# A gated mix of an S4 convolution and a dense branch, forward and backward: one row layout, the dense branch in three parts, S4 tables in place, transposes by DMA

## The chip, the cores and the metric

The kernel runs on one core of a Trainium2 chip. The metric is the device time of one execution in microseconds (us). The kernel before took 1587.69 us, the median of three runs (1584.29 to 1588.03). One execution was also recorded by the hardware profiler, and all rows below come from that one.

## What is computed

The input `u` has 2048 rows of 448 channels. A gate `g` (one number per row) mixes two branches, and the kernel returns the output and the gradients of all parameters:

```python
g = sigmoid((u * gate_w).sum(-1))
# branch a: a state-space convolution (S4), N = 256 complex modes per channel
K[d, l] = Re( sum_n  C[d,n] * exp(dt[d] * A[d,n] * l) * dt[d] * B[d,n] )
a = irfft(rfft(u padded) * rfft(K padded))[:L] + u * Dskip
# branch b: dense, 448 -> 1792 -> 448
b = relu(u @ w1 + b1)**2 @ w2 + b2
out = g * a + (1 - g) * b        # and the vjp of this for grad_out
```

The gradients need two more convolutions (`dK` from `u` and `g * grad_out`, `du` from `K` and `g * grad_out`), two sums S and T per channel and mode over the gradient `dK`, and six matrix products in place of the dense branch's two.

## The kernel before, in words

The whole program is one function of straight-line code. A planner orders the instructions of each engine before the run: the program's order is the priority, an instruction that the planner thinks ready may pass one that is not, a `high_priority` block goes ahead, and at run time each engine and each DMA queue takes its list strictly in order. Buffers come from pools. A pool that is opened after another has been closed gets the same memory, so its first use waits for the last use of the old one.

The stages, in the program's order:

1. Gate (L586 to L603) and S4 parameters (L291 to L349, transposed by TensorE). Rows of `u` lie as `(lt p)`, row `128*lt + p` on partition `p`, so `g * grad_out` goes out to DRAM and comes back in the layout of the transform.
2. Forward transforms of `u` and `g * grad_out` (`fwd1`, `fwd2`, each a set of matmuls with a trip through DRAM between, `gd`), the product of the spectra (`cmul_spec`), and the inverse (`inv1`, `inv2`, with a trip through `hd`), which gives `dK`.
3. S4 (L649 to L664): 14 chunks of 32 channels. For each pair of chunks `multipliers` makes sines and exponentials on VectorE and ScalarE. `build` then makes two tables by doubling, `Y` (6 levels) and `XW` (5 levels), each level three VectorE operations (L392 to L394). `Y` has two buffers and `build` has high priority, so the tables of chunk c+1 are made beside the use of chunk c. `kgen` makes the filter K, `back` transposes the tables on TensorE (L461, L471), copies them out of PSUM on ScalarE (L462, L474), multiplies by `dK` (L480), copies (L483), makes two products per group of channels on VectorE (L489, L490) and sums them by matmuls with a selection matrix (L499).
4. Transform of K, the parameters' gradients (L699 to L758), two products of spectra and two inverses, stored as `y_d` and `du_d`.
5. The dense branch (L780 to L932), in two halves of 896 hidden units. Its products need `h` and its gradient in both orientations, so `h` is transposed on TensorE and the hidden gradient is computed twice (L897, L908). Each half runs seven loops of matmuls one after another. Its pools are opened after the transforms' are closed.
6. The tail (L940 to L1011): loads of `grad_out`, `y_d`, `du_d`, and whole-tensor VectorE operations for output and input gradient.

All DMAs are issued from the queues of SP and ACT; POOL issues none.

Of the kernel before, what the change touches and what calls it, by code (L numbers as in the profile page):

```python
# [2 lines left out]

# [9 lines left out]
ALU = mybir.AluOpType  # L13
# [66 lines left out]
class FFTCtx:  # L80
    def __init__(self, tc, cpool, wpool, stg, psum, dram_consts=None):
        self.tc = tc
        self.nc = tc.nc
        nc = self.nc
        self.wpool = wpool
        self.stg = stg
        self.psum = psum
        if dram_consts is None:
            hc = host_consts()
            dram_consts = {name: (nc.inline_tensor(arr, name=f"c_{name}"), arr.shape) for name, arr in hc.items()}  # L90
        self.dram_consts = dram_consts
        self.c = {}
        for i, (name, (dr, shp)) in enumerate(dram_consts.items()):
            class _A:
                shape = shp
            arr = _A
            with tc.tile_pool(name=f"cld_{name}", bufs=1) as cld:
                t32 = cld.tile([P, arr.shape[1]], fp32, name=f"c32_{name}")
                (nc.sync if i % 2 == 0 else nc.scalar).dma_start(t32[:], dr.ap())
                tb = cpool.tile([P, arr.shape[1]], bf16, name=f"cb_{name}")  # L100
                nc.vector.tensor_copy(tb[:], t32[:])
            self.c[name] = tb
        self.evac_i = 0

    def dma(self):
        self.dma_i = getattr(self, "dma_i", 0) + 1
        return self.nc.sync if self.dma_i % 2 == 0 else self.nc.scalar

    def evac(self, dst, src):
        nc = self.nc  # L110
        if self.evac_i % 3 != 2:
            nc.scalar.copy(dst, src)  # L112
        else:
            nc.vector.tensor_copy(dst, src)
        self.evac_i += 1

    @staticmethod
    def tl_dram(ap2d):
        t = ap2d.tensor
        off = ap2d.offset  # L120
        return bass.AP(tensor=t, offset=off, ap=[[16 * D, 4], [64 * D, 32], [1, 16 * D]])

    def tl_load(self, dst_tile3, src_dram2d):
        for g in range(4):
            src = bass.AP(tensor=src_dram2d.tensor, offset=src_dram2d.offset + 16 * g * D, ap=[[64 * D, 32], [1, 16 * D]])
            self.dma().dma_start(dst_tile3[32 * g:32 * g + 32].rearrange("p a d -> p (a d)"), src)

    def tl_store(self, dst_dram2d, src_tile3):
        for g in range(4):
            dst = bass.AP(tensor=dst_dram2d.tensor, offset=dst_dram2d.offset + 16 * g * D, ap=[[64 * D, 32], [1, 16 * D]])  # L130
            self.dma().dma_start(dst, src_tile3[32 * g:32 * g + 32].rearrange("p a d -> p (a d)"))

    def fwd1(self, src_dram2d, gd, pool, tag="xs"):
        nc = self.nc
        c = self.c
        xs = pool.tile([P, 16, D], bf16, tag=tag, name=tag)
        self.tl_load(xs, src_dram2d)
        F1 = c["F1BD"]
        for hh in range(2):
            for q in range(4):  # L140
                st = self.stg.tile([P, 4, D], bf16, tag="st", name="st_g")
                for j2 in range(2):
                    ps = self.psum.tile([P, 2, 512], fp32, tag="ps", name="ps")
                    for jj in range(2):
                        j0p = q * 4 + j2 * 2 + jj
                        nc.tensor.matmul(ps[:, jj, 0:D], lhsT=F1[:, hh * 128:(hh + 1) * 128], rhs=xs[:, j0p, :], start=True, stop=True)
                    self.evac(st[:, 2 * j2:2 * j2 + 2, :], ps[:, :, 0:D])
                j0base = 32 * hh + q * 4
                for g2 in range(2):
                    dst = bass.AP(tensor=gd, offset=(j0base + 16 * g2) * 64 * D,  # L150
                                  ap=[[D, 64], [64 * D, 4], [1, D]])
# [890 lines left out]
```

## Time and profile before

| | before |
|---|---|
| profiled execution, device time | 1587.86 us |
| its span, first to last instruction | 1586.1 us |
| mean granted TensorE clock | 0.757 of full speed |
| median of 3 runs | 1587.69 us |

The rows give start or busy times in us, and the mean of one instruction in ns. Busy time of overlapping instructions on an engine is counted once, while the mean is of each instruction alone, so a mean times a count can exceed the busy time. A queue (SPq, ACTq) is where an engine issues DMAs. "Idle before" is how long an engine stood before such instructions, and what ended the wait.

### The profile page before, as it was taken

The page shows a single profiled execution, that of the slowest core. Times are in us where ns is not written, and L with a number is a line of the kernel's source. Part 1 is how long each engine was busy: PE and PEld are TensorE (multiplying, and loading weights), DVE is VectorE, ACT ScalarE, POOL GpSimd, SP SyncE. Part 2 cuts the span into 40 slices and gives each one's busy share as a digit, 9 for nine tenths or more (in the row PEclk, how much of TensorE's full clock was granted, in tenths as well). Part 3 has the DMA queues.
Part 4 walks back from the last instruction along what each step waited for, and adds up shares of the span by engine and source line. Part 5 has one row for each costly group of instructions (what it writes and reads, how often), then busy time and mean ns, then how long its engine had stood idle before and what let it go on. Part 6 is the DMA issues. An engine that isn't in the chain of part 4 may idle for free. (4 is left out here: it accounts for less than half of the span.)

```text
span 1586.1 us, 22870 instructions
## 1 busy us (share of the span) xinstructions
PE 860.7 (54%) x9553; PEld 500.8 (32%) x9568; DVE 1041.7 (66%) x1432; ACT 753.1 (47%) x976; POOL 38.4 (2%) x97
## 2 busy tenths in 40 slices
PE   0243410464656656575656231123499999999911
PEld 0111100343444434454444110000255455444500
DVE  3422834999999999999994269831225720766267
ACT  0033471585858586876654253113173636245042
POOL 0000000000000000000000000000000000000000
PEclk9966655577786768777887655555599999999965
DMA  6576448000000000000002753499501000000042
GB/s 148 132 239 212 202 113 187 1 2 8 2 9 1 8 2 8 2 2 8 2 8 51 195 184 133 151 121 253 170 21 33 9 21 1 1 21 6 17 139 93
DMA packets 92302, 115.53 MB, mean 73 GB/s; under 512 B 18019, under 2 KB 88678, under 8 KB 90278
## 3 DMA queue, kind: packets, MB, share of 16 engines
q1 hardware_dynamic: 52854, 57.43, 14.1%
q10 hardware_dynamic: 39344, 56.63, 11.5%
q8 instruction: 75, 1.23, 0.3%
q14 instruction: 29, 0.24, 0.1%
HBM read 65.41 MB, written 48.63 MB: 72 GB/s over the span
## 5 line engine op out<-in xcount | busy, mean ns | idle before, releaser
L499 PE MATMUL sps<-P,sel 128*32 128x256 bf16 x896 | 149.3, 323 | 70.6 <-DVE P L490 39.6
L499 PEld LDWEIGHTS <-sel 128*32 128x32 bf16 x896 | 95.0, 111 | 114.1 <-issue 88.5
L483 ACT CAST zb<-psz 128x1024 bf16<-128x1024 f32 x112 | 111.1, 1028 | 22.2 <-PE psz L480 21.9
L474 ACT COPY yts<-ytp 128x1024 bf16<-128x1024 bf16 x112 | 109.4, 1031 | 11.3 <-PE ytp L471 11.1
L433 PE MATMUL psk<-Y,XW 128*32 128x64 bf16 x1792 | 31.0, 241 | 114.2 <-DVE XW L394 112.4
L471 PE MATMUL ytp<-identb,Y 128*64 128x128 bf16 x1792 | 87.4, 243 | 8.7 <-ACT XT L462 8.7
L480 PE MATMUL psz<-yts,DK 64*32 64x256 bf16 x896 | 48.5, 368 | 68.6 <-ACT yts L474 67.6
L489 DVE TENSOR_TENSOR P<-zb,XT 128x2048 bf16<-128x2048 bf16 x56 | 68.4, 1221 | 25.3 <-ACT zb L483 25.1
L392 DVE TENSOR_TENSOR U<-Y,PRY 128x128 bf16<-128x128 bf16 (+2 forms) x84 | 72.9, 868 | 14.8 <-POOL Y L404 11.8
L471 PEld LDWEIGHTS <-Y 128*64 128x64 bf16 x1792 | 67.2, 123 | 35.4 <-issue 34.0
L394 DVE TENSOR_TENSOR Y<-U,V 128x128 bf16<-128x128 bf16 (+2 forms) x84 | 73.1, 870 | 2.2
L393 DVE TENSOR_TENSOR V<-Y,PIY 128x128 bf16<-128x128 bf16 (+2 forms) x84 | 72.4, 862 | 0.0
L394 DVE TENSOR_TENSOR XW<-U,V 128x256 bf16<-128x256 bf16 (+4 forms) x70 | 70.2, 1003 | 0.9
L392 DVE TENSOR_TENSOR U<-XW,PRX 128x256 bf16<-128x256 bf16 (+4 forms) x70 | 69.9, 999 | 0.7
L393 DVE TENSOR_TENSOR V<-XW,PIX 128x256 bf16<-128x256 bf16 (+4 forms) x70 | 69.8, 997 | 0.0
L490 DVE TENSOR_TENSOR P<-zb,XT 128x2048 bf16<-128x2048 bf16 x56 | 68.4, 1222 | 0.0
L433 PEld LDWEIGHTS <-XW 128*32 128x32 bf16 x1792 | 28.0, 124 | 120.5 <-issue 120.0
L186 PEld LDWEIGHTS <-cb_MI 64*128 64x128 bf16 x192 | 13.2, 119 | 161.5 <-issue 135.0
L186 PE MATMUL ps<-PcY,cb_MI 64*128 64x448 bf16 x64 | 14.8, 560 | 90.6 <-ACT st_h L112 36.5
L112 ACT CAST st_g<-ps 128x896 bf16<-128x896 f32 x33 | 29.0, 907 | 70.4 <-DMA gd<-st_g 38.2
L112 ACT CAST st_h<-ps 128x896 bf16<-128x896 f32 x32 | 28.0, 904 | 68.6 <-DMA hd<-st_h 47.7
L437 ACT CAST Kall<-psk 128x512 bf16<-128x512 f32 x14 | 8.2, 585 | 104.6 <-PE psk L433 104.6
(253 smaller groups left out, 2009.0 us busy)
## 6 DMA issues: line engine op xcount, KB each, us to landing
Gn<-in_grad_out_dram ACTq DMA_DIRECT2D x3, 1792.0 KB, 12.7
gd<-st_g SPq DMA_DIRECT2D x24, 224.0 KB, 3.1
gd<-st_g ACTq DMA_DIRECT2D x24, 224.0 KB, 3.9
hd<-st_h SPq DMA_DIRECT2D x12, 448.0 KB, 4.6
hd<-st_h ACTq DMA_DIRECT2D x12, 448.0 KB, 5.9
hs<-hd SPq DMA_DIRECT2D x12, 448.0 KB, 7.0
hs<-hd ACTq DMA_DIRECT2D x12, 448.0 KB, 9.4
c_M<-c_M ACTq DMA_DIRECT2D x2, 2048.0 KB, 8.2
```

The lines of the kernel that those rows point to most:

```text
L112: nc.scalar.copy(dst, src)
L392: nc.vector.tensor_tensor(out=U, in0=lo, in1=bcast_dims(pr, [0, (None, n), 1]), op=ALU.mult)
L393: nc.vector.tensor_tensor(out=V, in0=rev_dim(lo, 3), in1=bcast_dims(pi, [0, (None, n), 1]), op=ALU.mult)
L394: nc.vector.tensor_tensor(out=hi, in0=U, in1=V, op=ALU.add)
L433: nc.tensor.matmul(ps[32 * g:32 * g + 32, 0, i * 64:(i + 1) * 64], lhsT=XW[:, W2 + w, :, 1 - t], rhs=Y[:, w, :, t], start=(k == 0), stop=( ...
L471: nc.tensor.transpose(ytp[64 * t:64 * t + 64, ii, h * P:(h + 1) * P], Y[:, w, :, t], self.identb[:], tile_position=(0, 64 * t))
L474: nc.scalar.copy(yts[:], ytp[:])
L480: nc.tensor.matmul(psz[32 * ii:32 * ii + 32, t, 256 * s:256 * s + 256], lhsT=(DK[64 * t:64 * t + 64, :, d] if s == 0 else DKB[64 * t:64 * ...
L483: nc.scalar.copy(zb[:, :, :, i2, :], psz[:].rearrange("p t (s n) -> p t s n", s=2))
L489: nc.vector.tensor_tensor(out=P1[:].rearrange("p t s g n -> p t s (g n)"), in0=zv, in1=xb, op=ALU.mult)
L490: nc.vector.tensor_tensor(out=P2[:].rearrange("p t s g n -> p t s (g n)"), in0=zv, in1=rev_dim(xb, 1), op=ALU.mult)
L499: nc.tensor.matmul(sps[32 * g:32 * g + 32, r, 0:256], lhsT=self.sel[:, k, off:off + 32], rhs=Q[:, t, s, i2, :], start=first, stop=last, ti ...
```

## The change

Nearly every line is rewritten. What it does, part by part:

1. **One layout.** Rows lie as the transform wants them (partition `32*g + l1` holds the 16 rows `64*l1 + 16*g + t`) from the first load to the last store, also in the dense branch. The trip of `g * grad_out` through DRAM, `y_d` and `du_d` go. Constants come as bf16.
2. **S4 multipliers once, ahead.** For each of the 14 chunks a record of all 11 levels is made before the transforms' products, stored to DRAM and loaded again by its chunk. The first two values of each doubling come from the record, so `XW` has 4 levels and `Y` has 5.
3. **Tables in place.** `Y` and `XW` have one buffer each, for all chunks; `build(c+1)` writes where `kgen(c)`, `tables_t(c)` and the loads of chunk c read. `build` has no priority over `back`.
4. **Y transposed by DMA.** Four transposing DMAs per chunk, 512 KB each, from the SP queue, into three rotating buffers, replace 128 transposes on TensorE and eight copies on ScalarE. `kgen` and the transposes of `XW` share one PSUM bank.
5. **Dense branch in three parts.** Part 1 (hidden units and their gradient, once each, transposed layout, stored to DRAM) stands behind the first transforms in the program and must end before S4 begins, since S4's `Y` and `XW` use the memory of its inputs. Part 2 (gradients of w1 and w2, with 28 transposing loads of 512 KB from DRAM) and part 3 (output of the branch and its input gradient) stand behind S4 and the K transform in the program, but use memory and PSUM banks that are free during S4.
6. **Tail inside the inverses.** The two last inverses add the skip term, the dense branch and the gate's gradient by further matmuls into the same PSUM tile, and VectorE and ScalarE write the outputs from it.
7. **POOL issues DMAs**: records, spectra, weights, hidden units, K, S and T, the parts of the dense branch.

The core of the diff (left out: the classes `FFTCtx` and `S4`, whose bodies are shown above, the transforms, which are the same matmuls on quarters of a spectrum, and the gradients of the parameters):

```diff
-    tcp0_ctx = ExitStack()
-    T = S4(tc, tcp0)
+    UT = K.t("Y16", [P, LT, DT, P])
+    DBT = K.t("X16", [P, LT, DT, P])
+    for (dst, src) in ((UT, U), (DBT, DB)):
+        for q in range(4):
+            nc.sync.dma_start_transpose(out=dst[:, 4 * q:4 * q + 4].rearrange("p t a b -> p (t a) b"),
+                                        in_=src[:, 4 * q:4 * q + 4, :].rearrange("p t d -> p (t d)"))
+    K.fwd1(lambda j: U[:, j, 0:D], gd[0])
+    K.fwd1(lambda j: DA[:, j, :], gd[1])
...
+    for c in range(NCH):
+        tw = K.t("F17", [P, 4, NLEV, W2], fp32)
+        v, s, q_, e = (tw[:, i] for i in range(4))
+        rec = K.t("rec", [P, NF, W2])
+        V.tensor_tensor(out=v, in0=Tt[:, c]..., in1=pow2[:]..., op=ALU.mult)
+        V.tensor_scalar(out=s, in0=v, scalar1=MAGIC, scalar2=MAGIC, op0=ALU.add, op1=ALU.subtract)
+        V.tensor_tensor(out=v, in0=v, in1=s, op=ALU.subtract)
+        S.activation(s, v, ACT.Sin, scale=2 * math.pi)
+        S.activation(q_, v, ACT.Sin, scale=math.pi)
+        S.activation(q_, q_, ACT.Square)
...
+        V.scalar_tensor_tensor(out=rec[:, 0:NLEV], in0=q_, scalar=-0.5, in1=e, op0=ALU.add, op1=ALU.mult)
+        V.tensor_tensor(out=rec[:, NLEV:2 * NLEV], in0=s, in1=e, op=ALU.mult)
...
+        G_.dma_start(dst, rec[:].rearrange("p f w -> p (f w)"))
...
+    for jp in range(FT // 2):
...
+            for lc in range(4):
+                ps = K.ps(NT[nti % 4], [P, 512])
+                for dt in range(DT):
+                    T_.matmul(ps[:], lhsT=w1t[0:k, dt, jj * P:jj * P + P], rhs=UT[0:k, 4 * lc:4 * lc + 4, dt, :], ...)
+                S.activation(rT[:, 512 * lc:512 * lc + 512], ps[:], ACT.Relu, bias=b1_f[:, j:j + 1])
+            V.tensor_tensor(out=h2, in0=rT, in1=rT, op=ALU.mult)
+            G_.dma_start(bass.AP(tensor=hT_d, offset=j * P * L, ap=[[L, P], [1, L]]), h2)
...
+    Y = K.t("Y16", [P, W2, 2, 64])
+    XW = K.t("X16", [P, 2, W2, 32, 2])
+    def double(T3, n, T4, rev, pr, pi):
...
+        V.tensor_tensor(out=hi, in0=lo, in1=bcast_dims(pr, [0, (None, n // 2), 1]), op=ALU.mult)
+        V.tensor_tensor(out=Vv..., in0=lo, in1=bcast_dims(pi, [0, (None, n // 2), 1]), op=ALU.mult)
+        V.tensor_tensor(out=T4[:, :, :, n:2 * n], in0=T4[:, :, :, n:2 * n], in1=V4, op=ALU.add)
+    def tables_t(c):
+        for gp in range(2):
+            for gg in range(2):
+                pt = K.ps("X", [P, 4, 256], bf16)
...
+                S.copy(XT[:, gg].rearrange("p t i n -> p (t i n)"), pt[:].rearrange("p a n -> p (a n)"))
+    def load_yt(g):
+        YT = RB[:, 3 + yi % 3].rearrange("p (h i n) -> p h i n", h=2, i=CW)
+        nc.sync.dma_start_transpose(out=YT.rearrange("p h i n -> p (h i) n"), in_=Y[:, 16 * g:16 * g + 16].rearrange("p w t b -> p (w t b)"))
...
+    for c in range(NCH):
+        build(c)
+        kgen(c)
+        XTs = tables_t(c)
+        back(c, XTs, [load_yt(g) for g in range(3)])
...
+    for j in range(FT):
+        for w in range(2):
+            hh = hn[:, (2 * j + w) % 4]
+            nc.sync.dma_start_transpose(out=hh, in_=bass.AP(tensor=src, offset=j * P * L, ap=[[L, P], [1, L]]))
+            for t in range(LT):
+                T_.matmul(ps[:, 0:width], lhsT=hh[:, t, :], rhs=(DB2[:, t, :] if w == 0 else U[:, t, 0:D + 1]), ...)
...
+    for lb in range(LT // 2):
...
+            G_.dma_start(hb, bass.AP(tensor=(hT_d if w == 0 else dhT_d), offset=256 * lb, ap=[[L, P], [P * L, FT], [1, 256]]))
...
+            K.inv2(hs, q, x, ps, lambda t: [(ident[:], A[:, t, :]), (negI[:], BR[:, t, 0, :])])
+                V.scalar_tensor_tensor(out=jk[:], in0=ps[:, hp, 0:D], scalar=1.0, in1=Gt[:, t, :], ..., accum_out=dg[:, t:t + 1])
+                V.scalar_tensor_tensor(out=A[:, t, :], in0=ps[:, hp, 0:D], scalar=g32[:, t:t + 1], in1=BR[:, t, 0, :], ...)
```

## Rows read from the trace of the kernel before

**Rows 1.** Busy time by stage: window, us, PE, PEld, DVE, ACT, POOL, PEclk, DMA, GB/s.

```profile
0.00:80.00 80.00, 9.18 (x32) 5.16 (x32) 33.83 (x95) 5.57 (x10) 1.55 (x10) 1.00 0.58 139
80.00:262.00 182.00, 59.34 (x320) 22.46 (x320) 74.42 (x78) 78.46 (x90) 1.51 (x7) 0.59 0.61 187
262.00:878.00 616.00, 357.36 (x6720) 262.77 (x6720) 579.17 (x640) 406.17 (x444) 31.84 (x80) 0.75 0.06 13
878.00:1135.00 257.00, 64.28 (x368) 22.36 (x369) 129.04 (x215) 71.54 (x114) 0.84 (x1) 0.53 0.69 186
1135.00:1505.00 370.00, 357.91 (x2066) 183.62 (x2081) 171.77 (x370) 164.29 (x270) 2.64 (x2) 0.99 0.05 14
1505.00:1586.00 81.00, 12.65 (x49) 4.46 (x48) 53.48 (x37) 27.05 (x48) 0.00 (x0) 0.62 0.33 114
```

**Rows 2.** The chain that ended last, its shares of the span by engine (page, part 4).

```profile
PE 21%; DVE 4%; ACT 1%; DMA 1%; issue 1%; DVEq 0%; ACTq 0%
```

**Rows 3.** Busy time in one chunk of S4, columns as in rows 1.

```profile
343.00:384.00 41.00, 23.94 (x486) 18.23 (x484) 40.41 (x45) 23.53 (x27) 2.36 (x8) 0.79 0.03 8
```

**Rows 4.** Groups on VectorE during S4 by shape: busy us, mean ns, idle before.

```profile
L489 DVE TENSOR_TENSOR P<-zb,XT 128x2048 bf16<-128x2048 bf16 x56 | 68.4, 1221 | 25.3 <-ACT zb L483 25.1
...
L392 DVE TENSOR_TENSOR U<-XW,PRX 128x256 bf16<-128x256 bf16 x14 | 5.2, 371 | 0.1
...
L372 DVE TENSOR_TENSOR tA<-tB,tD 128x640 f32<-128x640 f32 x6 | 4.9, 819 | 0.0
...
L372 DVE TENSOR_TENSOR tA<-tB,tD 128x768 f32<-128x768 f32 x5 | 4.8, 959 | 2.4 <-ACT tD L371 2.4
```

**Rows 5.** Timeline within one chunk of S4: start, duration, instruction.

```profile
549.99 1.94 PE L433 MATMUL psk<-Y,XW 128*32 128x64 bf16 x128 [9.44 <-DVE XW L394]
...
551.86 1.89 PE L461 MATMUL xtp<-identb,XW 128*128 128x128 bf16 x16
...
551.99 0.59 ACT L437 CAST Kall<-psk 128x512 bf16<-128x512 f32 x1 [10.83 <-PE psk L433]
...
552.93 1.93 ACT L462 COPY XT<-xtp 128x1024 bf16<-128x1024 bf16 x2 [0.35 <-PE xtp L461]
...
557.93 0.37 PE L480 MATMUL psz<-yts,DK 64*32 64x256 bf16 x8 [0.28 <-ACT yts L474]
...
558.66 1.06 ACT L483 CAST zb<-psz 128x1024 bf16<-128x1024 f32 x1
```

**Rows 6.** DMA issues: queue, count, KB each, median us from issue to landing.

```profile
Gn<-in_grad_out_dram ACTq DMA_DIRECT2D x3, 1792.0 KB, 12.7
...
hd<-st_h SPq DMA_DIRECT2D x12, 448.0 KB, 4.6
...
hs<-hd ACTq DMA_DIRECT2D x12, 448.0 KB, 9.4
...
s_d<-stS SPq DMA_DIRECT2D x28, 64.0 KB, 1.7
```

**Rows 7.** Groups in the dense stage, 1135 to 1505 us.

```profile
L854 PE MATMUL ps<-uT,w1h 128*128 128x512 bf16 x215 | 51.7, 380 | 0.4
...
L912 DVE SCALAR_TENSOR_TENSOR r_l<-dh2b,r_l 128x448 bf16<-128x448 bf16 x64 | 39.3, 625 | 10.0 <-ACT dh2b L911 3.7
...
L856 ACT ACTIVATE rT<-ps,b_f 128x512 bf16<-128x512 f32 x56 | 37.5, 686 | 10.3 <-PE ps L854 10.1
```

**Rows 8.** Groups in the stage of the K transform, 878 to 1135 us.

```profile
L112 ACT CAST SP_K<-ps 128x896 bf16<-128x896 f32 x11 | 9.4, 910 | 0.4 <-PE ps L165 0.4
...
L527 DVE TENSOR_TENSOR cm<-SPx,SP_K 128x1792 bf16<-128x1792 bf16 x8 | 8.7, 1090 | 5.0 <-DMA SPx<-sp_d 5.0
...
L718 DVE TENSOR_TENSOR x<-Wr,ST 128x256 f32<-128x256 f32 (+1 forms) x12 | 5.1, 424 | 0.6 <-ACT ob_dBi L746 0.2
```

**Rows 9.** Groups on ScalarE, whole span: sines of the multipliers.

```profile
L367 ACT ACTIVATE tC<-tA 128x768 f32<-128x768 f32 x7 | 5.9, 844 | 0.1
```

**Rows 10.** Timeline of the first stage: the gate's first operation, and its wait.

```profile
25.51 3.89 DVE L590 TENSOR_TENSOR prod<-Un,gw_bc 128x7168 bf16<-128x7168 bf16 x1 [8.60 <-DMA Un<-in_A_u_dram]
```

More of the change, by code (lines that the diff above doesn't have):

```diff
@@ L20 @@
 P = 128
-L, D = 2048, 448
+L, D, N, F = 2048, 448, 256, 1792
+LT = L // P
+FT = F // P
+DT = 4
+DSZ = [128, 128, 128, 64]
+DP = 512
+CW = 8
+NG = 4
+CC = NG * CW
+NCH = D // CC
+GC = 2
+W2 = 2 * CC
+NLEV = 11
+NF = 26
+MAGIC = 12582912.0
 def host_consts():
@@ L512 @@
[L512 to L534 removed]
+        self.pool = pool
@@ L944 @@
-    for lt in range(LT):
-        nc.vector.tensor_scalar(out=DA_n[:, lt, :], in0=Gn[:, lt, :], scalar1=g32[:, lt:lt + 1], scalar2=None, op0=ALU.mult)
-    Yn = fin1.tile([P, LT, D], bf16)
-    nc.sync.dma_start(Yn[:], y_d.ap().rearrange("(lt p) d -> p lt d", p=P))
-    DUn = fin1.tile([P, LT, D], bf16)
-    nc.scalar.dma_start(DUn[:], du_d.ap().rearrange("(lt p) d -> p lt d", p=P))
-    row = small.tile([1, 4, D], fp32)
-    ps = psA.tile([P, 512], fp32, tag="ps", name="ps")
-    for lt in range(LT):
-        nc.tensor.matmul(ps[0:1, 0:D], lhsT=ones_b[:, 0:1], rhs=DB_n[:, lt, :], start=(lt == 0), stop=(lt == LT - 1))
@@ L955 @@
-    nc.vector.tensor_copy(row[:, 0, :], ps[0:1, 0:D])
-    with tc.tile_pool(name="tmp2", bufs=1) as tmp2:
-        dau = tmp2.tile([P, LT, D], bf16)
-        nc.vector.tensor_tensor(out=dau[:], in0=DA_n[:], in1=Un[:], op=ALU.mult)
-        ps = psA.tile([P, 512], fp32, tag="ps", name="ps")
-        for lt in range(LT):
-            nc.tensor.matmul(ps[0:1, 0:D], lhsT=ones_b[:, 0:1], rhs=dau[:, lt, :], start=(lt == 0), stop=(lt == LT - 1))
-        nc.vector.tensor_copy(row[:, 1, :], ps[0:1, 0:D])
@@ L990 @@
-    gp = small.tile([P, LT], bf16)
-    nc.vector.tensor_tensor(out=gp[:], in0=g_b[:], in1=omg_b[:], op=ALU.mult)
-    ds_b = small.tile([P, LT], bf16)
-    nc.vector.tensor_tensor(out=ds_b[:], in0=dg_b[:], in1=gp[:], op=ALU.mult)
-    ds32 = small.tile([P, LT], fp32)
-    nc.vector.tensor_copy(ds32[:], ds_b[:])
-    ps = psA.tile([P, 512], fp32, tag="ps", name="ps")
-    for lt in range(LT):
-        nc.tensor.matmul(ps[0:1, 0:D], lhsT=ds_b[:, lt:lt + 1], rhs=Un[:, lt, :], start=(lt == 0), stop=(lt == LT - 1))
@@ new lines @@
+    GU = K.t("Y16", [P, LT, D])
+    V.tensor_tensor(out=GU[:], in0=Gt[:], in1=Ut[:], op=ALU.mult)
+    row = K.t("st", [1, 3, D], bufs=2)
+    ps = K.ps("N0", [P, 512])
+    for t in range(LT):
+        T_.matmul(ps[0:1, 0:D], lhsT=omg_b[:, t:t + 1], rhs=Gt[:, t, :], start=(t == 0), stop=(t == LT - 1))
+    S.copy(row[:, 0], ps[0:1, 0:D])
+    nc.sync.dma_start(out_13.rearrange("(o d) -> o d", o=1), row[:, 0])
+    ps = K.ps("N1", [P, 512])
+    for t in range(LT):
+        T_.matmul(ps[0:1, 0:D], lhsT=g_b[:, t:t + 1], rhs=GU[:, t, :], start=(t == 0), stop=(t == LT - 1))
@@ L1015 @@
+    ps = K.ps("N0", [P, 512])
+    for t in range(LT):
+        T_.matmul(ps[0:1, 0:D], lhsT=ds_b[:, t:t + 1], rhs=Ut[:, t, :], start=(t == 0), stop=(t == LT - 1))
+    S.copy(row[:, 2], ps[0:1, 0:D])
+    nc.sync.dma_start(out_14.rearrange("(o d) -> o d", o=1), row[:, 2])
 _INS = ['A_u', 'A_A_re', 'A_A_im', 'A_B_re', 'A_B_im', 'A_C_re', 'A_C_im', 'A_log_dt', 'A_Dskip', 'B_x', 'B_w1', 'B_b1', 'B_w2', 'B_b2', 'gate_w', 'grad_out']
```

1407 lines of the change are left out of this document (619 added, 788 removed).

## The prediction

> **What bounds the kernel now.** I read the busy time by stage first [rows 1]. Six windows cover the span, and they run one after another. S4, 616 us, is VectorE's: it is busy 579 of them, and a single chunk shows 40.4 of 41.0 us [rows 3]; the chunks that follow repeat this. The dense stage, 370 us, is TensorE's (358 busy, granted clock 0.99), and VectorE and ScalarE are less than half busy in it. The two transform stages, 182 and 257 us, are nobody's: no engine is busy for more than half of either, the DMA share is 0.6 to 0.7, the clock 0.59 and 0.53, so they wait for trips through DRAM. The tail, 81 us, is a line of VectorE operations. The chain that ended last [rows 2] reaches back only through the tail and the dense stage (TensorE 21% of the span), so it says nothing of S4; I go by the windows. In each stage some engine stands idle that another stage needs, and what the change can win is overlap.
>
> The profiled execution took 1587.86 us, 1.8 us more than its span and 0.2 us more than the median of 1587.69, so a sum made against the span needs 1.8 us added and nothing more.
>
> **Part 1, up to S4 (before: 262 us).** The gate can't start before its first load lands, at 25 us [rows 10]. It becomes 16 fused operations of 0.63 us [rows 7], 10 us in place of two large ones; about 40 us with the scalings. Its scaled rows no longer go out to DRAM and back. The records are new here, and they are a chain, since `tw` and `rec` have one buffer each: five VectorE operations on 704 fp32 elements, between 0.82 and 0.96 us [rows 4], take 4.5 us; three on ScalarE, a little under 0.84 us [rows 9], 2.4 us; the small ones on the path, as an estimate, 3 us. Ten us each, 14 of them, 140 us from about 35 on: 175 us. The products of the spectra use the same memory (`F17`), so they start only then; four quarters with their inverses, each six products of 1.09 us [rows 8] and the copies behind them, need 35 us: 210 us. Dense part 1 runs beside this: 448 matmuls at 0.24 us (busy time over count [rows 7]) are 107 us, with the transforms' 59 [rows 1] 166 on TensorE. ScalarE gets 59 copies of 0.91 [rows 8], 56 activations of 0.69 [rows 7], 56 copies that I price alike, and the records' 70: 200 us. VectorE gets the records' 78, 29 copies and 24 products of 1.09, dense 36, gate 20: 192 us. Both are near full, so I add 30 us for waits: the first build starts at 240 us. Bounds: 205, where the two engines run without a gap, and 300, where the records stretch by a half. The inverse that gives `dK` ends beside the first build; if it is late, chunk 0's matmuls wait up to 20 us.
>
> **S4 (before: 616 us).** VectorE's work per chunk falls: the multipliers' five tensor operations per pair of chunks (0.96 and 0.82 us [rows 4], half of the sum 4.5 us) and the first level of each table (six of at most 0.37 us) go. From 40.4 us that leaves 34 to 35; I take 35, since means overlap. But the tables now have one buffer, and the overlap of one chunk's use with the next one's tables goes. I count from the end of `Y(c)`. `kgen` takes 1.9 us, its copy 0.6; then the `XW` transposes in four rounds through one bank, each 0.95 us for eight (16 take 1.89) and 1.0 for the copy [rows 5]: 7.8 us; then four small start values, about 1.2 us. Only at 11.5 us may VectorE write `XW(c+1)`. What it has until then are products, and the first needs a transposing load, 0.4 us of matmuls and two copies of 1.06 [rows 5].
>
> Before has no transposing DMA and so no price for one of 512 KB. The nearest rows move plain pieces: 1792 KB in 12.7 us, so 3.6 us for 512 KB, below; 448 KB to landing in 4.6 us from SBUF and in 9.4 us into SBUF [rows 6], so 5.3 and 10.7 us, above. I take 5.3, since it is the row that starts from an SBUF tile on SP's queue. [...]
>
> So the first product starts at 8.3 us, and VectorE idles for that long in each chunk: 43.3 us. The fourth load waits for a free buffer and lands by 22 us, before `XW` is done at about 30, so it costs nothing; that cover is gone once loads take over 8 us. Behind those loads stand, on SP's queue, two transposing loads of dense part 2 per chunk, and on TensorE some 64 dense matmuls; for what they hold up I add 4 us: 47 us. ScalarE loses eight copies of Y and gains little. Bounds: 38.5 us (transposes of `XW` done before `kgen`, 3.5 us of idle time) and 57 us (below). The first build costs 26 us (35 less eight products of up to 1.22 us [rows 4]). S4: 26 + 13 x 47 = 637 us.
>
> **After the last table (before: 257 + 370 + 81 us).** Dense parts 2 and 3 are 896 matmuls, 215 us at 0.24 us. TensorE was idle 17 us of each chunk [rows 3], 238 us in all, and loses the 128 transposes of Y, so I cost them at nothing here; without that cover, see the second rival. The remaining path: the last chunk's four loads 21 us; K read back in pieces of 256 bytes, 20 us (between 12.7 and 4 x 9.4 [rows 6]); first transform stage 25 us (half of its copies wait for two PSUM buffers instead of four; 16 to 35); DRAM trip 10 us; four quarters of 12 products and four copies at 1.09 us on VectorE, 17.5 us each, 70 us; last store 5 us. Parameter gradients: 4 x 31 operations at 0.42 us [rows 8], 52 us, of which I put 22 in the waits and 30 on the path. Tail: first load 9, first inverse with 32 fused operations of 0.63 us [rows 7] and waits 23, second inverse eight steps of about 4 us, 32, last store 5. Sum 151 + 30 + 69 = 250 us; bounds 190 and 338, the two windows of before [rows 1].
>
> **Sum.** 240 + 637 + 250 + 1.8 = 1129 us, 459 us less than before. The dense stage is 370 of that.
>
> **Rivals.**
> 1. *S4's gap closes.* The planner puts the `XW` transposes ahead of `kgen`, since they need only `XW`: 38.5 us per chunk, 1129 - 13 x 8.5 = 1018 us. For it: one priority order, and nothing else ready on TensorE then. Against it: the shared bank.
> 2. *The dense parts don't go under S4.* They stand behind it in the program, and if the planner finds no room or a list built on wrong durations stalls, they follow S4: 896 matmuls at 0.38 us (the mean of one, when they don't run densely [rows 7]) are 340 us from 877 on, then the load of their result 13 and the inverses 60: about 1290 us. Part 3 alone (170 us) would be hidden by the K transform.
> 3. *Queues hold S4 up.* SP's list, TensorE's and POOL's are in order: a dense transposing load or matmul whose data is late stands before a load of `Y`, a `kgen` or a record. One extra load of 10 us per chunk in the way makes 57 us: 1259 us. For it: 84 transposing loads of 512 KB on one queue; POOL's DMAs have no row at all.
> 4. *Slower: the transposing loads take their time block by block.* A load has 16 blocks of 128x128. If each cost what the smallest row shows, 1.7 us for 64 KB [rows 6], a load takes 27 us, the next `Y` (13 us) waits for four of them, and a chunk takes 121 us. With y us per load the total is 666 + 56y: 2178 us, and slower than before from y = 16.5 us, three times the price I took and half again the highest plain row. [...] Against it: the plain rows move a whole tile in the time of a few small ones, so blocks should overlap.
>
> **How the numbers follow.** Forecast 0.46, rival 1 0.13, rival 2 0.13, rival 3 0.20, rival 4 0.07; 0.01 for what I don't see. The range runs from below rival 1 to above rivals 2 and 3 with part 1 at its upper bound: 1010 to 1400 us; rival 4 is left out. A measurement of this kernel can tell about 0.3% from no change. Faster by more: 0.91; within: 0.01; slower: 0.08.
>
> **What would show it.** S4: `kgen` copies 47 us apart, with VectorE idle some 8 us ahead of the first product or of `XW`; 4 transposing loads each about 5 us. Dense matmuls of parts 2 and 3 inside S4's window, and the granted clock there above 0.75. The first build at 240 us, held by the records' chain. The prediction is wrong if a transposing load takes over 10 us, if the tail waits for the dense branch's result, or if ScalarE's list, not the records, sets the first stage.

## The result and the profile after

The changed kernel takes 1355.57 us (median of 4 runs, 1349.27 to 1360.10) against 1587.86 us: a ratio of 0.854 (95% interval 0.850 to 0.858), 232 us less. The forecast was 1129 us, 459 us less; the time lies inside its range, and the gain is half of what it stated. The profiled execution is one of 1360.10 us, with a span of 1358.3 us.

Busy time by stretch, kernel after (columns as in [rows 1]). The stretches are divided at the first build of the tables (288.5 to 328.4) and, from there on, at the copies of `kgen` (chunk 0, chunks 1 and 2, chunk 3, chunks 4 to 12, and what follows the last copy):

```profile
0.00:288.50 288.50, 183.72 (x692) 53.90 (x693) 182.86 (x315) 168.46 (x318) 46.10 (x94) 0.89 0.75 215
288.50:328.40 39.90, 8.24 (x76) 1.99 (x76) 32.39 (x32) 16.47 (x22) 2.56 (x5) 0.50 0.69 191
328.40:411.80 83.40, 47.28 (x609) 24.79 (x608) 37.52 (x35) 35.28 (x55) 5.15 (x9) 0.70 0.93 165
411.80:521.80 110.00, 91.75 (x1023) 49.20 (x1022) 74.50 (x70) 52.40 (x86) 20.38 (x34) 0.91 0.85 172
521.80:635.20 113.40, 54.66 (x512) 26.30 (x510) 37.51 (x35) 26.65 (x41) 16.96 (x24) 0.71 0.97 131
635.20:1115.90 480.70, 221.67 (x3492) 128.69 (x3491) 337.59 (x315) 192.15 (x261) 41.07 (x69) 0.65 0.39 81
1115.90:1358.00 242.10, 118.82 (x688) 38.89 (x688) 163.07 (x301) 67.02 (x84) 4.48 (x9) 0.59 0.73 189
```

The dense stage of [rows 1] is gone: its parts 2 and 3 run from 369 to 737 us, in S4's time. But S4 has become longer: VectorE, full before [rows 3], is busy 337.59 of 480.70 us in the nine chunks from 4 on, and 37.51 of 113.40 us in chunk 3 alone. The time went into waits in S4 and into a late start of it; the stretch behind S4 came out as forecast.

One of the chunks without dense work, kernel after, timeline (columns as in [rows 5]) and busy time:

```profile
950.50 2.29 DVE L555 TENSOR_TENSOR Y<-Y,F 128x4096 bf16<-128x4096 bf16 x1
952.85 1.96 PE L593 MATMUL psX<-Y,X 128*32 128x64 bf16 x128 [26.32 <-DVE Y L555]
952.94 11.14 SPq L622 DMA_TRANSPOSE R<-Y  x4
954.87 0.59 ACT L597 CAST st<-psX 128x512 bf16<-128x512 f32 x1 [3.01 <-PE psX L593]
959.22 0.47 PE L642 MATMUL psF<-R,K 64*32 64x256 bf16 x8 [4.42 <-DMA R<-Y]
959.84 1.03 PE L613 MATMUL psX<-ident,X 128*128 128x128 bf16 x8
964.98 2.36 DVE L654 TENSOR_TENSOR P<-R 128x2048 bf16<-128x2048 bf16 x2 [12.19 <-ACT R L645]
966.20 1.01 PE L613 MATMUL psX<-ident,X 128*128 128x128 bf16 x8 [0.49 <-ACT R L614]
977.56 0.42 DVE L549 TENSOR_TENSOR X<-X,F 128x512 bf16<-128x512 bf16 x1
1005.00 2.29 DVE L555 TENSOR_TENSOR Y<-Y,F 128x4096 bf16<-128x4096 bf16 x1
...
954.87:1009.37 54.50, 19.43 (x352) 11.89 (x352) 37.50 (x35) 20.64 (x27) 1.11 (x2) 0.53 0.30 49
```

`Y` ends at 952.8. The bank of the `XW` transposes is free from 955.5 on, yet they start at 959.84: on TensorE's queue they stand behind matmuls on `YT`, the transposed `Y`, which wait for the first load until 959.22. So the first product waits 12.19 us, the eight products (9.8 us of work) spread over 14 us behind the copies of ScalarE, and the next `XW` starts 25 us after `Y`'s end.

Longer stalls stand in chunk 0, in chunk 3 and at the start of chunk 4. Timelines, kernel after, of these three (four, four and three rows); in the distances between copies of `kgen` below, the last two both count as chunk 3:

```profile
328.39 14.00 SPq L622 DMA_TRANSPOSE R<-Y  x1
342.73 2.16 SPq L522 DMA_DIRECT2D K<-dk_d  x1
362.53 0.69 PE L642 MATMUL psF<-R,K 64*32 64x256 bf16 x16 [30.43 <-DMA K<-dk_d]
367.62 2.36 DVE L654 TENSOR_TENSOR P<-R 128x2048 bf16<-128x2048 bf16 x2 [39.26 <-ACT R L645]
...
522.84 28.67 SPq L802 DMA_TRANSPOSE D<-in_B_w_dram  x2
523.19 1.10 POOL L799 DMA_DIRECT2D U<-in_B_w_dram  x1
551.61 9.01 SPq L622 DMA_TRANSPOSE R<-Y  x3
562.02 2.36 DVE L654 TENSOR_TENSOR P<-R 128x2048 bf16<-128x2048 bf16 x2 [41.73 <-ACT R L645]
...
608.62 13.80 SPq L622 DMA_TRANSPOSE R<-Y  x3
626.77 4.73 PE L821 MATMUL psN<-D,S 128*128 128x448 bf16 x14 [7.53 <-DMA S<-dhT_d]
633.72 0.47 PE L593 MATMUL psX<-Y,X 128*32 128x64 bf16 x34
```

In chunk 0 `dK` lands only at 362; half of it was issued behind a transposing load that held SP's queue for 14 us. The two halves of that load, from the view of DMA issues (columns as in [rows 6]):

```profile
K<-dk_d ACTq DMA_DIRECT2D x1, 1792.0 KB, 25.8
K<-dk_d SPq DMA_DIRECT2D x1, 1792.0 KB, 19.8
```

So the hold is the smaller part of this wait: ACT's half, issued at 326.38, had 25.8 us to go by itself and landed at 352.17, 10 us ahead of SP's. In `e7`, below, both halves are issued at 319.8, behind no such hold, and take 22.5 and 25.1 us. In chunk 3 the loads of `Y` stand on SP's queue behind two transposing loads of dense part 3's weights (28.67 us of issue, a load of 1568 KB by POOL beside them). In chunk 4 `kgen`, ready at 608.5, stands on TensorE's queue behind dense matmuls whose block lands at 626.77.

The first stage, kernel after: busy time of three stretches, then the first operation and the end of the first record, the end of the last one, and the products of the first three quarters of the spectrum, each by its first operation:

```profile
0.00:40.00 40.00, 6.72 (x16) 2.07 (x17) 19.46 (x72) 6.66 (x8) 6.61 (x27) 1.00 0.99 200
40.00:80.00 40.00, 19.41 (x54) 5.35 (x53) 17.69 (x29) 14.37 (x19) 1.31 (x2) 1.00 1.00 204
160.00:200.00 40.00, 39.56 (x148) 11.38 (x146) 33.75 (x58) 37.64 (x83) 12.82 (x21) 1.00 0.58 198
...
67.17 0.88 DVE L418 TENSOR_TENSOR F<-P,pow 128x704 f32<-128x704 f32 x1
100.06 0.22 DVE L435 TENSOR_TENSOR rec<-F 128x64 bf16<-128x64 f32 x1
223.57 0.22 DVE L435 TENSOR_TENSOR rec<-F 128x64 bf16<-128x64 f32 x1
223.82 1.09 DVE L202 TENSOR_TENSOR F<-K 128x1792 bf16<-128x1792 bf16 x1
246.64 1.09 DVE L202 TENSOR_TENSOR F<-K 128x1792 bf16<-128x1792 bf16 x1 [1.72 <-ACT K L159]
264.35 1.09 DVE L202 TENSOR_TENSOR F<-K 128x1792 bf16<-128x1792 bf16 x1 [0.66 <-ACT K L159]
```

For 80 us the DMA engines are full, and no other engine is busy for half of it; by 160 us TensorE is full (39.56 of 40 us) and ScalarE nearly (37.64). The first record takes from 67 to 100 us, the other 13 take 9.5 us each. The products start as the last record ends, and a quarter takes 17.7 us (the first one 22.8).

### The profile page after: what moved, and what is told of

Its sections match the earlier page's. It is cut to its first block, busy times and chain, and to the rows that moved or that the text cites. A ratio compares the mean times of both kernels' runs of the same rounds, so it can differ in the third digit from the quotient of the medians.

```text
span 1358.3 us, 17800 instructions
## 1 busy us (share of the span) xinstructions
PE 726.1 (53%) x7088; PEld 323.8 (24%) x7088; DVE 865.4 (64%) x1102; ACT 558.4 (41%) x865; POOL 136.7 (10%) x244
## 3 DMA queue, kind: packets, MB, share of 16 engines
q1 hardware_dynamic: 252280, 96.03, 37.4%
## 5 line engine op out<-in xcount | busy, mean ns | idle before, releaser
L654 DVE TENSOR_TENSOR P<-R 128x2048 bf16<-128x2048 bf16 x112 | 133.9, 1223 | 307.4 <-ACT R L645 296.2
L645 ACT CAST R<-psF 128x1024 bf16<-128x1024 f32 x112 | 115.2, 1051 | 43.1 <-PE psF L642 34.2
L159 ACT CAST st<-psF 128x896 bf16<-128x896 f32 x69 | 60.8, 909 | 111.2 <-PE psF L220 56.1
L663 PE MATMUL psS<-P,cb_sel 128*32 128x256 bf16 x896 | 91.2, 321 | 19.5 <-DVE P L654 19.3
L614 ACT COPY R<-psX 128x1024 bf16<-128x1024 bf16 x56 | 56.9, 1015 | 58.3 <-PE psX L613 58.2
L555 DVE TENSOR_TENSOR Y<-Y,F 128x256 bf16<-128x256 bf16 (+4 forms) x70 | 70.5, 1007 | 2.4
L549 DVE TENSOR_TENSOR Y<-Y,F 128x256 bf16<-128x256 bf16 (+4 forms) x70 | 70.4, 1006 | 1.9
L550 DVE TENSOR_TENSOR F<-Y,F 128x256 bf16<-128x256 bf16 (+4 forms) x70 | 69.7, 995 | 0.4
L549 DVE TENSOR_TENSOR X<-X,F 128x512 bf16<-128x512 bf16 (+3 forms) x56 | 64.8, 1158 | 1.9 <-ACT F L567 0.5
L550 DVE TENSOR_TENSOR F<-X,F 128x512 bf16<-128x512 bf16 (+3 forms) x56 | 64.5, 1151 | 1.9 <-ACT F L568 1.9
L555 DVE TENSOR_TENSOR X<-X,F 128x512 bf16<-128x512 bf16 (+3 forms) x56 | 64.8, 1156 | 1.4
L663 PEld LDWEIGHTS <-cb_sel 128*32 128x32 bf16 x896 | 52.4, 109 | 54.4 <-issue 45.0
L161 DVE CAST st<-psF 128x896 bf16<-128x896 f32 x27 | 29.4, 1089 | 51.0 <-DMA gd<-st 26.4
L613 PE MATMUL psX<-ident,X 128*128 128x128 bf16 x448 | 52.7, 291 | 11.7 <-ACT R L614 10.7
L220 PE MATMUL psF<-P,cb_MI 64*128 64x448 bf16 x128 | 28.8, 560 | 56.1 <-DVE P L204 25.1
L642 PE MATMUL psF<-R,S 64*32 64x256 bf16 x896 | 57.5, 365 | 0.5 <-ACT S L631 0.5
```

The costliest lines, as they stand in the source:

```text
L549: V.tensor_tensor(out=hi, in0=lo, in1=bcast_dims(pr, [0, (None, n // 2), 1]), op=ALU.mult)
L550: V.tensor_tensor(out=Vv.rearrange("p (x a q) -> p x a q", x=rows, q=2), in0=lo, in1=bcast_dims(pi, [0, (None, n // 2), 1]), op=ALU.mult)
L555: V.tensor_tensor(out=T4[:, :, :, n:2 * n], in0=T4[:, :, :, n:2 * n], in1=V4, op=ALU.add)
L613: T_.transpose(pt[:, 2 * t + i2, h * P:(h + 1) * P], XW[:, t, w:w + 4, :, 0].rearrange("p w a -> p (w a)"), ident[:])
L614: S.copy(XT[:, gg].rearrange("p t i n -> p (t i n)"), pt[:].rearrange("p a n -> p (a n)"))
L642: T_.matmul(psz[32 * ii:32 * ii + 32, t, 256 * s:256 * s + 256], lhsT=(DK[64 * t:64 * t + 64, :, d] if s == 0 else DKB[64 * t:64 * t + 64, ...
```

## The experiments

Each kernel differs from the changed kernel by the edit shown. Only the changed kernel and `e12_all` were run four times; every other time is of a single run, so the table goes by stretches of the traces: the first copy of `kgen`, the distances from one such copy to the next (us), and the rest of the span. Chunk 3 is noisy: in `e3`, `e4`, `e10` and `e11`, whose edits lie elsewhere, it took 80 to 96 us, not 113. I count no difference in it as a gain of theirs. The start varies too: in `e11`, whose edit lies behind S4, the records end at 237 us instead of 224 and the first copy comes 14 us late. And the first two columns go together: in `e1` the matmuls of the first `kgen` end at 330.6 as before, but its copy stands on ScalarE's queue behind an operation that waits for `dK` until 359.8. The wait that the changed kernel has in chunk 0 lies ahead of the first copy in `e1`, so the two columns are to be compared by their sum (411.8 us in the changed kernel, 407 in `e1` and `e2`, 394 to 397 in `e7` to `e9` and `e12`).

| kernel | time | first | chunk 0 | 1, 2 | 3 | 4 to 12, mean | rest |
|---|---|---|---|---|---|---|---|
| changed, profiled | 1360.1 | 330 | 81 | 56, 54 | 113 | 53.4 | 242 |
| e1_xw_early | 1289.0 | 362 | 46 | 54, 47 | 77 | 51.1 | 242 |
| e2_xw_pipelined | 1268.8 | 362 | 45 | 48, 49 | 75 | 49.1 | 245 |
| e3_records_first | 1317.2 | 327 | 70 | 56, 59 | 80 | 53.3 | 244 |
| e4_bulk_beside_loads | 1357.3 | 332 | 81 | 54, 55 | 86 | 55.9 | 245 |
| e5_part3_paced | 1291.5 | 332 | 79 | 53, 55 | 52 | 52.8 | 243 |
| e6_y_by_tensore | 1285.3 | 330 | 72 | 48, 48 | 72 | 51.4 | 251 |
| e7_ordered | 1240.5 | 351 | 45 | 47, 49 | 81 | 46.5 | 247 |
| e8_ordered_paced | 1227.1 | 351 | 44 | 50, 47 | 62 | 46.0 | 257 |
| e9_ordered_tensore | 1162.0 | 351 | 43 | 39, 41 | 40 | 42.8 | 262 |
| e10_quarters_ahead | 1318.6 | 316 | 80 | 56, 55 | 89 | 52.7 | 247 |
| e11_no_param_grads | 1334.5 | 344 | 80 | 54, 55 | 96 | 52.9 | 227 |
| e12_all | 1162.6 | 358 | 39 | 40, 41 | 42 | 42.2 | 261 |

**The order on TensorE's queue.**

```
     for c in range(NCH):
-        build(c)
-        kgen(c)
+        rec = build_x(c)          # the levels of XW
         XTs = tables_t(c)
+        build_y(rec)              # the levels of Y
+        kgen(c)
         back(c, XTs, [load_yt(g) for g in range(3)])
```

> Edit: the sixteen transposes of XW and their four copies are written between the building of XW and the building of Y, so they no longer stand on TensorE's queue behind the first matmuls on YT; nothing else changes. Theory A (in the chunks without dense work, 53.5 to 54.5 us each, VectorE waits 12 us for its first product because the XW transposes wait in line behind matmuls that wait for the first transposing load, and XW of the next chunk waits for those transposes): the first product starts about 9 us after Y's end, the first levels of the next XW run before it, a quiet chunk takes 44 to 46 us, the whole 1225 to 1260 us. Rival B (the load of 6 us and ScalarE's copies set the chunk by themselves): a quiet chunk stays at 52 us or more, the whole above 1320 us.

One quiet chunk of it, busy time and the first product (`Y` ended at 949.0):

```profile
951.04:998.79 47.75, 19.38 (x352) 12.66 (x352) 37.41 (x35) 21.52 (x28) 5.01 (x10) 0.50 0.35 62
...
958.05 2.36 DVE L657 TENSOR_TENSOR P<-R 128x2048 bf16<-128x2048 bf16 x2 [2.62 <-ACT R L648]
```

The same 37.4 us of VectorE's work now take 47.75 us, and the first product starts 9.0 us after `Y`. A quiet chunk is 6.5 us shorter; that is two thirds of what A stated, so the order is the larger cause of the long chunk and not the only one. The whole missed A's range by 29 us: chunk 3 still takes 77 us, and chunk 5 takes 80, where TensorE stands 20.5 us before a load of `Y`.

```
+    build_x(0), tables_t(0)
     for c in range(NCH):
+        build_y, kgen(c), three loads of Y
+        build_x(c + 1), tables_t(c + 1)
         back(c, ...)
```

> Edit: as the edit before (XW's transposes right behind XW), and XW of the next chunk is written ahead of the products of this one, so that VectorE has 14 us of work while the loads of Y land. Theory A: VectorE is idle only for the 2.5 us of kgen and its copy; a quiet chunk takes 40 to 42 us, the whole 1180 to 1215 us. Rival B (the loads, 3 us of issue each on one queue and 4.3 us to land, four per chunk, keep the next Y waiting): a quiet chunk takes 46 us or more, the whole above 1250 us.

In this kernel part of the products read the next chunk's `XW` tables, since a table's buffer is written over; the work and its sizes are the same. A quiet chunk takes 47.4 us, B's number. VectorE waits 3.9 us for the start values of `XW` and 5.0 us for the last load of `Y`: the first operation of the next `Y` stands in the middle of its list. That is again an order, so I fixed the order by hand:

```
+        build_x(c + 1)                            # VectorE: XW,
+        products of g = 0, 1, 2 behind it         # six products,
+        tables_t(c + 1), build_y behind these     # Y,
+        kgen(c + 1), three loads of Y
+        products of g = 3 behind Y                # two products
```

> Edit on the changed kernel: records first as in e3_records_first; XW of the next chunk ahead of the products of this one, its transposes behind the products, VectorE's order fixed as XW, the products of g = 0 to 2, Y, the two products of g = 3; nothing added or left out. In e1_xw_early and e2_xw_pipelined a quiet chunk took 47.5 us: VectorE, with 38 us of work, waited 3.9 us for the start values of XW behind kgen and some 5 us for the last load of Y, because the first operation of Y stood in the middle of XW. Theory A (order alone): the last load lands 14 us after Y's end, well before XW and six products are done, and the two late products fill the wait for kgen: a quiet chunk takes 40 to 43 us, the whole 1150 to 1185 us. Rival B (something else holds 47 us, ScalarE's copies or the loads): a quiet chunk stays at 46 us or more, the whole above 1220 us.

A quiet chunk, busy time:

```profile
865.20:907.92 42.72, 16.55 (x353) 11.09 (x352) 37.37 (x36) 21.38 (x29) 5.05 (x10) 0.58 0.39 69
```

The last four chunks take 41.3 to 43.2 us, as A stated: the loads of `Y` do not bound S4 once the order lets other work cover them. The whole missed by 55 us, for the chunks with dense work stayed at 47 to 53 us and chunk 3 at 81.

**The loads that were slow.**

```
+        if c in (8, 9, 11, 12):     # on POOL, behind k_d<-st
+            dma(bulk_d, B_w2)       # 1792 rows of 896 bytes
```

> Edit: in chunks 8, 9, 11 and 12, which have no dense work, POOL issues a copy of 1568 KB in rows of 896 bytes from DRAM to DRAM (result not used) right behind its store of K, beside the transposing loads of Y; added work, nothing left out. Theory A (the loads that took 14 to 28 us in chunks 0 and 3 were slow because a bulk load was in flight, not because of their own form): the transposing loads of these four chunks land in 10 us or more instead of 4.3 and each of the chunks grows by 8 to 25 us; the whole 1390 to 1450 us. Rival B (the bulk transfers run beside them at no cost, and the slow loads were slow by their source or destination): these chunks grow by less than 3 us; the whole within 1350 to 1368 us.

Time from issue to landing of the loads of `Y` in chunk 11 (three of the four have a landing on record), first in the changed kernel, then in this one:

```profile
DMA to landing us min/median/max: 5.1/6.0/6.2
```

```profile
DMA to landing us min/median/max: 6.6/16.9/17.9
```

In this chunk the loads slow down by up to three times, as A stated; in chunks 8, 9 and 12 the slowest on record takes 10.6 to 10.7 us. But against the same chunks of the changed kernel they grow by 3.7 to 5.1 us in these three cases and by 10 us in chunk 11, so A holds for the loads and, but for chunk 11, not for the chunks, and the whole (1357 us) is B's: most of the delay falls on the second and third load, which the products reach late. A bulk transfer beside the loads explains loads of 14 us, not a stall of 42.

```
+    weights: loads behind the last Y load of chunk 4 / the record load of chunk 5
+    block lb: load behind the record load of chunk 5 + lb,
+              matmuls behind the last reduction of chunk 5 + lb
```

> Edit on the changed kernel: dense part 3 gets fixed places. Its weights are loaded behind chunk 4's last load of Y (the transposing ones) and behind the load of chunk 5's record (the plain one), its blocks are loaded behind the record loads of chunks 5 to 12, and TensorE does a block behind the last reduction of chunks 5 to 12, ahead of the next kgen; no work is added or left out. Theory A (the 113 us between two kgens, chunk 3, are 32 us in which loads of Y stood on SP's queue behind the transposing loads of the weights, and 25 us in which kgen stood on TensorE's queue behind matmuls of part 3 whose block had not landed): no chunk after the first takes over 62 us, the whole 1285 to 1310 us. Rival B (what the dense part costs S4 it costs wherever it stands, by DMA traffic and TensorE's time): the eight chunks with a block grow by 5 us or more each, the whole above 1330 us.

No chunk after the first takes over 55 us; chunk 3 falls from 113 to 52 us, and the eight chunks with a block take 51.7 to 54.4 us. So dense part 3 costs S4 nothing by itself; what it cost chunk 3 were places in two queues: 61 us against the profiled execution of the changed kernel, 28 against the shortest chunk 3 of a kernel whose edit lies elsewhere (`e3`, 80 us). In `e8` the same pacing on the ordered kernel:

> Edit: e7_ordered with dense part 3 paced as in e5_part3_paced. Theory A (the stalls of chunks 3 and 4 are of the queues' order and go with the pacing; the gaps of TensorE still hold the 12 us of a block per chunk): 40 to 60 us less than e7_ordered, the whole 1095 to 1135 us. Rival B (in a chunk of 42 us TensorE has no gap for a block, and reductions or kgen wait for it): the eight chunks with a block take 50 us or more, the whole within 20 us of e7_ordered.

It gained 13 us: chunk 3 fell from 81 to 62 us, but the chunks with a block take 42 to 47 us (the last four, quiet before, 1.5 to 4.4 us more) and the rest of the span is 10 us longer. B was nearer by the whole, though the chunks stayed below its 50 us. In chunk 3 three transposing loads of part 2 hold SP's queue, which they share with those of `Y`, for 19.26 us, and `kgen`'s matmuls take from 538 to 554 us with gaps for which the trace names no wait; what holds this chunk is not shown.

**The transposing DMA itself.**

```
     def load_yt(g):
-        nc.sync.dma_start_transpose(YT, Y[16 g : 16 g + 16])
+        for h in range(2):                       # bank X
+            8 x T_.transpose(pt[:, i], Y[16 g + 8 h + i], ident)
+            S.copy(YT[:, h], pt)
```

> Edit on the changed kernel: the four loads of YT per chunk are taken back to TensorE, sixteen transposes each in two rounds through the one PSUM bank of the XW transposes and two copies on ScalarE (as in the kernel before, which had more banks for it). Theory A (with one bank and ScalarE for all the copies, 12 rounds of 2 us per chunk stand in line, so the transposing DMA pays although VectorE waits for it): a quiet chunk takes 57 to 66 us instead of 54, the stall of 32 us in chunk 3 goes, the whole 1370 to 1450 us. Rival B (the wait for the load is what makes the chunk long): a quiet chunk takes 46 to 52 us, the whole below 1310 us.

A was wrong. With the transposes back on TensorE, the rest of the change as it is, the kernel is 70 us faster than the changed one: chunks of 48 us where dense work keeps TensorE busy, 52 to 53 us later, no load of `Y` on SP's queue. Against the profiled execution the gain is 75 us: 42 are chunk 3's, which is noisy, the other chunks are 42 us shorter together, and the rest of the span is 8 us longer. The part of the change that was named for S4 costs time.

> Edit: e8_ordered_paced with the loads of YT taken back to TensorE as in e6_y_by_tensore (sixteen transposes and two copies each, through the one PSUM bank); SP's queue then holds no work of S4 but the dense parts'. Theory A (the transposing DMA has no worth of its own here; it ties S4 to SP's queue): chunk 3 falls from 62 to 50 us or less, the others stay between 42 and 48 us, the whole 1190 to 1220 us. Rival B (in the ordered kernel the loads are hidden, and 12 rounds of 2 us through one bank with eight more copies on ScalarE are not): most chunks take 50 us or more, the whole above 1245 us.

In the ordered kernel too, and more: 65 us off `e8`. Every chunk but one takes 39 to 43 us; chunk 5, beside the loads of part 3's weights, takes 57. Chunk 10 of this kernel and of `e8`, both with a dense block in it, and one of the changed kernel with dense part 2:

```profile
775.17:816.64 41.47, 29.69 (x475) 18.68 (x474) 37.26 (x36) 30.02 (x40) 8.38 (x14) 0.87 0.27 77
```

```profile
828.85:875.90 47.05, 29.91 (x411) 15.88 (x410) 37.35 (x36) 23.18 (x32) 8.39 (x14) 0.72 0.51 112
```

```profile
468.19:521.76 53.57, 45.55 (x512) 24.40 (x512) 37.26 (x35) 25.86 (x43) 9.95 (x15) 0.90 0.79 166
```

VectorE has 37.3 us of work in all three and is busy 90% of the first. Against the changed kernel's chunk the granted clock is not what tells them apart: it is 0.87 and 0.90 of full speed. Against `e8` the clock rose with the transposes, from 0.72 to 0.87, and how much of the 5.6 us is the clock's, how much the queue's and how much the loads' own landing, no run separates.

**The stages around S4.**

```
-    loads of U and DB, first transforms, parameters and records
+    parameters and records, loads of U and DB, first transforms
```

> Edit: the loads of the parameters and the 14 records are written ahead of the transposing loads of U and DB and of the first transform stage; nothing is added. Theory A (the first record took from 67 to 100 us because its loads stood on SP's queue behind those and its operations behind copies that waited for stores; the other 13 take 9.5 us each): the records end by about 185 us instead of 224, and the first kgen comes at 285 to 300 us instead of 328; the whole 1315 to 1330 us. Rival B (dense part 1 holds the memory of the tables and TensorE until 243 us, and what the records gain it loses): the first kgen moves by less than 12 us, the whole stays within 1340 to 1360 us.

The whole came out as A stated, but not by A's way: the records end at 208 us, the last product of the quarters moves from 287 to 280 us only, the first `kgen` by 4 us, the second by 16 us. The other 33 us are chunk 3's, which this edit does not touch. B holds for the start of S4: dense part 1's last store moves from 244 to 289 us.

```
+        nxt = spectra(q + 1)        # second transform of the next quarter
         cmul(Pc, qs[1], qs[0]); inv1(Pc, q)
+        qs = nxt
```

> Edit on the changed kernel: in the first stage the second transform of the next quarter is written ahead of the products and the inverse of this one; nothing added or left out. Theory A (a quarter took 17.7 us and not the 8.75 us of the forecast because transform, products and inverse follow one another through the two F banks in the order written): a quarter takes 10 to 13 us, the last product ends at 262 to 275 us instead of 288, the second kgen comes at 382 to 398 us instead of 410, the whole 1328 to 1345 us. Rival B (the loads of the quarters from DRAM, or the copies on ScalarE and VectorE, set the 17.7 us): the last product ends after 283 us, the whole within 1348 to 1362 us.

The four quarters' products take 45 us from first to last instead of 64, the last ends at 275 us, and the second `kgen` comes 16 us earlier. A holds for the quarters, at the upper end of its range. The gain at the start is about as large as the 14 us by which `e11` shows the start to vary, but it comes from the quarters: the records end later here (229 us); of the 37 us in the whole, 24 are chunk 3's.

> Edit: e9_ordered_tensore with the quarters of the first stage as in e10_quarters_ahead; nothing left out. Theory A (the two act on different stretches): 10 to 20 us off the stretch before S4 and nothing else moves, the whole 1138 to 1156 us. Rival B (in this kernel the records end earlier and dense part 1 and the loads of dK hold the start of S4): within 6 us of e9_ordered_tensore, 1156 to 1168 us.

This kernel takes 1162.64 us (4 runs, 1152.36 to 1162.90), a ratio of 0.730 (0.726 to 0.734) to the kernel before. B was right. The quarters' products end at 246 us, 33 us earlier than in `e9`, but the last store of dense part 1 is issued here (`e9`: 287.70):

```profile
326.32 0.53 POOL L524 DMA_DIRECT2D dhT_d<-R  x1 [3.17 <-DVE R L523]
```

The tables of S4 use the memory of dense part 1's inputs, so the first build waits for its last matmuls (they release the first write to `XW` at 324.91, and `XW`'s first doubling operation is at 327.13), and the first copy of `kgen` comes at 358 us. What one part of the first stage gains on the shared engines, another loses.

**Behind S4.**

```
-        31 operations of the parameter gradients per block of rows
+        memset of their outputs
```

> Edit on the changed kernel: the arithmetic of the parameter gradients behind S4 (4 x 31 operations) is left out and zeros are stored in its place; its loads and stores stay. The forecast put 30 of its 52 us on the path. Theory A (VectorE is busy 48.8 of the 50 us from 1200 on, so all of it lies on the path but what fills VectorE's waits before): the stretch from the last kgen to the end falls from 244 us to 195 to 215 us, the whole 1305 to 1330 us. Rival B (the DRAM trips of the K transform and the inverses set this stretch, and the operations lie in their waits): the stretch stays above 230 us, the whole above 1340 us.

From the last `kgen` to the end, busy time:

```profile
1105.43:1332.70 227.27, 121.64 (x688) 39.78 (x688) 120.60 (x170) 59.33 (x68) 4.47 (x9) 0.58 0.70 195
```

VectorE has 42 us less to do than in the same stretch of the changed kernel, and the stretch is 15 us shorter: between A and B. Most of the gradients lie in waits that stay when they go.

## Why the prediction was half right

What it had right: the dense parts 2 and 3 went under S4 at no cost in most chunks (chunks 1 and 2, full of part 2, take 56 and 54 us, quiet ones 53), and the 370 us of the dense stage are gone. A transposing load takes 5.1 us in the median of the 35 with a landing on record (5.3 taken). Records take 9.5 us (10). The stretch after the last table takes 244 us (250): its terms were off by more than the sum, since the gradients cost 15 us of the path and not 30, so part of that agreement is luck.

Where the 231 us between the forecast and the profiled execution lie, by its terms (the copies of `kgen` come 2 us after the ends of the tables):

| term | forecast | measured | miss |
|---|---|---|---|
| start and first build | 240 + 26 | 288.5 + 40 | +62 |
| chunk 0 | 47 | 81 | +34 |
| chunk 3 | 47 | 113 | +66 |
| the other 11 chunks | 47 each | 53.7 each | +74 |
| after the last table | 250 | 244 | -6 |

- *Part 1.* The path was the one of the forecast: the records' chain, then the quarters, then the tables (the first product at 223.82, right behind the last record; the last one ends at 288.5). The step that failed is "140 us from about 35 on". The first record ended at 100 us, not 45: its loads stood behind eight transposing loads and the stores of the first transform, with the DMA share at 0.99 and 1.00. "Four quarters" in 35 us failed too: I counted engine time, and they ran in a line, 64 us (`e10` takes 19 us of it away). The measured start lies inside my bounds of 205 to 300. When the records or the quarters come earlier, another bound is right behind: dense part 1 then holds the start (`e3`, `e12`).
- *Chunk 0.* I wrote that a late `dK` costs up to 20 us and put nothing into the sum. Chunk 0 took 34 us more than the sum has for it, 28 more than a quiet chunk. The load of `dK` itself, up to 25.8 us to landing, is the larger part of that; the hold of SP's queue put its second half some 10 us behind the first.
- *The quiet chunk.* The step that failed is the count from `Y(c)`: I had the `XW` transposes directly behind `kgen`, and they waited for a load, behind matmuls on the same queue. VectorE idled 17 us of 54.5, not the 12 of the sum (8.3 and 4), and its work was 37.5 us, not 35. `e1` has the order of my rival 1, the transposes ahead of `kgen`, and its quiet chunks take 47 us, not the 38.5 of that rival; that this is the forecast's number is luck. Even with the next chunk's `XW` ahead of the products (`e7`) 41 to 43 us is what the order gives. Two sums were off besides: the terms of the first product's 8.3 us make 7.8 (5.3, 0.4 and twice 1.06), and those of ScalarE's 200 us in part 1 make 190.
- *Chunk 3.* This is rival 3, in its form (SP's queue, TensorE's queue, a late block), but it came once with 60 us and not in each chunk with 10. `e5` shows it: only the places of the same work changed, and the chunk takes 52 us.
- *Rivals 2 and 4* did not occur. Against rival 4: 4.3 us to landing for 16 blocks (each load with a landing on record in the quiet chunk above). My sign of being wrong, a load of over 10 us, came true beside other traffic: 19.1 us in chunk 0 and 26.4 us at the start of chunk 4. 512 KB in 4.3 us from issue to landing are 122 GB/s, and SP was held 2.8 us by each issue (11.14 us for four). My 5.3 us, from the row of a plain store, was close to the median of 5.1.
- *The clock.* I expected over 0.75 in S4. That held only where dense work kept TensorE busy (0.91 in chunks 1 and 2, but 0.71 in chunk 3); in a quiet chunk, with TensorE busy 19.43 of 54.50 us, the rows show 0.53 of full speed.

What stays open: why the weights' two loads took 28.67 us of issue in the changed kernel and 11.79 us in `e4`, with the same order up to there. In the first POOL's bulk load came 0.35 us behind the first of them, in the second 2.1 us; that they raced is argued, not shown. In `e7`, too, a load of the weights that was issued 0.66 us ahead of that bulk load took 28.77 us of issue. Open as well is what makes chunk 3 so uneven from kernel to kernel.

## What to carry to other kernels

In these kernels an instruction that waited for a DMA held up what was written behind it on its queue: in the quiet chunk the `XW` transposes started at 959.84, behind matmuls that waited for a load until 959.22, though their bank was free from 955.5 on, and with the order of `e1` a quiet chunk took 47.75 us instead of 54.50. So for each such instruction list what stands behind it and whether it needs that DMA at all, and set the order by hand where a list built on estimated durations could get it wrong. Overlapping a stage with another is worth what its engines leave free, but it puts two streams on every queue; give the second fixed places in the first one's gaps (`e5`: chunk 3 took 52 us, not the 80 to 96 us of `e3`, `e4`, `e10` and `e11`). Price a DMA that replaces work on an engine with time to spare with its issue, its landing and its neighbours on the queue, not by its bytes: here a load of 512 KB took 2.8 us of issue and 5.1 us to landing in the median, and up to 26.4 us beside other traffic, and without these loads `e6` was 70 us faster.

## What the runs showed of the hardware

- A transposing DMA of 512 KB from SBUF to SBUF held SP's queue for 1.8 to 4.7 us to issue (changed kernel, from 900 us on), and four in a row for 11.14 us; of 74 plain DMAs there on SP's queue all but one show 0.2 to 0.8 us (that one 1.46).
- Beside a bulk transfer of 1568 KB in rows of 896 bytes the same loads landed in 6.6 to 17.9 us instead of 5.1 to 6.2 (chunk 11, `e4` and the changed kernel).
- In chunk 11 of `e4` a load came 12 us later after its issue than in the changed kernel, and the chunk grew by 10 us; chunks 8, 9 and 12, with loads of up to 10.7 us, grew by 3.7 to 5.1 us.
